# A planned order for the first tile, fewer masks, and one run of matmuls for the steps of rows 16 apart

## The chip, the core and the metric

The kernel runs on one core of one Trainium2 chip. The metric is the device time of one execution in microseconds (us); lower is better. Before the change it is 602.31 us, the median of three runs (602.05 to 604.03).

## What is computed

Two blocks follow each other. The first is a linear recurrence (RWKV-6) over 768 steps for 4 batches times 8 heads with 48 channels each; the second is a two-layer network with an exact GELU.

```python
for t in range(768):                       # r, k, v, w: (4, 8, 768, 48)
    cur = einsum('bhd,bhe->bhde', u * k[t], v[t])
    y[t] = einsum('bhd,bhde->bhe', r[t], state + cur)
    state = w[t][..., None] * state + einsum('bhd,bhe->bhde', k[t], v[t])
x = y reshaped to (3072, 384)
h = x @ w_in                               # 384 x 2048
out = (0.5 * h * (1 + erf(h / sqrt(2)))) @ w_out    # 2048 x 384
```

The two weights arrive as 64-bit floats, carried as 64-bit integers, and are turned into 32-bit floats on the chip.

## The kernel before

**Tiles.** The 3072 rows are eight tiles of 384 rows (half a sequence of one batch). `attention(x, unit)` makes the recurrence of tile x, `mlp(x)` its network. Both are Python generators: each `yield` ends a piece of work. While the network of tile x-1 fills TensorE, the recurrence of tile x is woven in between its matmuls. The instructions of every engine run in the order in which the generators are advanced; nothing reorders them. For tiles 1 to 7 that order is a string of letters, `PLAN[x]`: "." advances `mlp(x - 1)`, "s" the recurrence of tile x, "f" that of the tile after it, "l" loads, "c" the weight conversion, "w" masks and sums of weights, "x" sums of the network's input. After the string the streams are run to their ends.

**Tile 0** has no network to lie under. It is cut into two units (two pairs of heads each), `units[0]` and `units[1]`, that are advanced in turn by loops at the end of the kernel function, with matmuls on zeros (`keep_warm`, L240) between. A unit multiplies the decays w of neighbouring steps into totals (`tot_sb`, L427); then at each of six levels h = 1, 2, 4 to 32 it makes products of k and r on TensorE (`d`, L468), scales r and k by the totals on VectorE (L515, at the last level L508), and copies the wanted part of the products into `a_sb` through a mask (L527) or, for h of 16 and 32, with ScalarE (L524). At level 1 the diagonal is made too (`diag`, from r times u by ScalarE, L417; its copy is L479). The blocks of k are then transposed (`kt_ps`, L680), products of k and v made (`kv_ps`, L706), the states chained on VectorE (L726, L721), and y is the sum of two groups of matmuls (`y_ps`, L747 and L791); small copies called fences (L757, L759) stand between those two. y goes to `xT`, the input of the network (L798, L814), in part by small DMAs (L821). Tile 1 does the same steps with one unit.

**Loads.** `load_first` (L166) brings r, k and w of tile 0: per unit one DMA for r and k (768 KB) and one for w (384 KB). `weight_in` (L219, L214) brings a piece of weights, `load_second` (L178) tile 1 in eight parts; a one-element memset on VectorE (L218, L177) ahead of each part holds the DMA back to its place in the order. All of these are issued by SyncE.

**Weight conversion.** There are 16 pieces. ScalarE makes two halves of each (L345, L346, in `prepare`), VectorE finishes it (L357, L359, L361, L365, in `finish`). Five raw pieces fit.

**Masks.** Early in the kernel VectorE makes masks for the levels h = 1, 2, 4, 8, 16 and for the diagonal (L254 to L262, tensor_scalar and compare); GpSimd makes index patterns (`iota`), clears `a_sb` (L266) and the two state buffers (L270), makes the identity, and later lays out `places` (L296 to L301). Masks for `quarters` (h = 4 and 16) are made in tile 1.

**Tiles 2 to 7** use `quarters()`: two levels, h = 4 and h = 16, each with 12 blocks made in three bursts of 5, 5 and 2 (L596). A burst takes one of two pairs of PSUM banks, so the third waits until the first is copied out. At h = 16 the copies are ScalarE's (L612, six a burst). Then r is scaled (L637), k is scaled (L644, L648), k is transposed in blocks on VectorE (L547) and moved by twelve small DMAs (L542), and `kv_ps` follows. Two more PSUM banks, `bank_u`, belong to `mlp`: its first layer accumulates in them (`u_ps`, L925). The first layer of the network is L1051 for tiles 0 and 1 and L925 later, the second layer L1197 for tile 0 and L1065 later.

Of the kernel before, what the change touches and what calls it, by code (L numbers as in the profile page):

```python
# [20 lines left out]
C = 64  # L21
# [9 lines left out]
FINE = 4  # L31
# [6 lines left out]
PLAN = {  # L38
    1: (
        "ccsc.cs...c.c.csccc.cs.sccc.l.csccccssc.cccs.c..cccs.sc.ccslcsc.scsclc.c.scssl.clc.wcsc.cc"  # L40
        "wsc.l.cs.cclcc.cc.wlwlcc.c.cwcs...wwfs..w...wfwl...s.w..f..wfw...wffffffffw"
    ),
    2: (
        ".......s.l.wsslw.swssss.s.s.sss.lssls.ssssssw..s.swl..w..ww.s.w.s.sslls.ll.slf.wfs..f.xxx."
        ".xx"
    ),
    3: (
        "ss.l....ss.ss...ls.sl.....s..s....sss.s..ss.ssss.ssl...ssls..ssss..ss...s.s..ls..sl..sslls"
        "f.s..fsf.fl.f.xx..xfxx"
    ),  # L50
    4: (
        "...s.s..ss...sl.s..s..l.ssl.ss.ssss.s.s.ss...sss..sssls.s.sls...s.s.l...slsls...sl.sf.fs.f"
        "xxx.lx...x"
    ),
    5: (
        "s.sl....s.s...slss...s.s.l...s....ssls.sls..s.ssssl.ss...ss.s.ss.sss..s.s.....s.ssls.s.l.l"
        "sf.s.ffs.ff..xx..xfxxl"
    ),
    6: (
        ".s..slss.......s.s.s...sll.ssls.sssssl..s.ss...sss..sssss....ssl..ss....slsss...lsl.sf...f"  # L60
        "xxl.xf..xx"
    ),
    7: (
        "s.s.s.s....s..ss.s...s...s.....ss.ss.s.ss.sss.ss...sss..ss.sssss.......s.s..sss.s..s.s...x"
        "xx..xx"
    ),
# [8 lines left out]
def kernel(  # L75
# [83 lines left out]
    def load_first():  # L159

        t = bufs[0]
        loaded[0] = [None, None]
        size = 3 * NP * T // units_of(0)
        for i in range(units_of(0)):
            for a, b in ((0, size * 2 // 3), (size * 2 // 3, size)):
                nc.sync.dma_start(out=t[:, i * size + a:i * size + b], in_=rkw[0, :, i * size + a:i * size + b])  # L166
# [37 lines left out]
    raws = []  # L204

    def weight_in(gate=False):

        if len(raws) < len(pieces):
            dst, src = pieces[len(raws)]
            raws.append(cv.tile([128, PIECE], I64, name="raw", bufs=AHEAD) if wide else None)  # L210
            if wide:
                dst = raws[-1].rearrange("p (a c) -> p a c", a=dst.shape[1])
            if not gate:
                nc.sync.dma_start(out=dst, in_=src)  # L214
                return
            for i in range(dst.shape[1]):
                if wide:
                    nc.vector.memset(dst[:, i].bitcast(U32)[:, 0:1], 0)  # L218
                nc.sync.dma_start(out=dst[:, i], in_=src[:, i])  # L219
                yield  # L220

    nc.sync.dma_start(out=u_sb, in_=u)
# [22 lines left out]
    masks = {h: const.tile([128, C // 2], U8, name=f"mask{h}") for h in LEVELS[:-1]}  # L245
# [5 lines left out]
    s_qs = {h: q_ints[0][:, i * C:(i + 1) * C] for i, h in enumerate((1,) + QUARTERS)}  # L251
# [3 lines left out]
    for h in LEVELS[:-1]:  # L255
# [9 lines left out]
    a_sb = const.tile([128, 2, NPART * NI, C], F32, name="a_sb")  # L265
    nc.gpsimd.memset(a_sb, 0.0)  # L266
# [8 lines left out]
    quarter = {h: [const.tile([128, (3 - a) * C // 4], U8, name=f"quarter{h}_{a}") for a in range(3)] for h in QUARTERS}  # L275
# [4 lines left out]
    for i, h in enumerate(QUARTERS):  # L280
# [38 lines left out]
    def conversion():  # L319
# [10 lines left out]
        for _ in weight_in():  # L330
            pass
# [5 lines left out]
    def prepare(upto):  # L337
        if not wide:
            return
        for i in range(len(halfway), min(upto, len(raws))):  # L340
# [28 lines left out]
    def attention(x, unit):  # L369
# [91 lines left out]
        def products(bs, right, width):  # L461
            d = pair("d")
            n = 0
            for b in bs:
                for i in range(NI):
# [5 lines left out]
                    n += 1  # L471
            return d[:, :, 0:n * width]
# [10 lines left out]
        def halves():  # L483

            for h in LEVELS:
                m = C // 2 // h
                if np_ < NPART:

                    d = products(range(np_), lambda z, b, i, p: rc[z, b, i, p], C)
# [8 lines left out]
                if x == 1:  # L498
                    yield
# [841 lines left out]
```

## Time and profile before

| | before |
|---|---|
| median of the runs | 602.31 us |
| profiled execution | 603.68 us, of it 601.8 us from the first to the last instruction (the span) |
| TensorE busy | 587.2 us (98%), x7442 |
| VectorE busy | 459.9 us (76%), x878 |
| ScalarE busy | 261.3 us (43%), x604 |
| GpSimd busy | 8.4 us (1%), x24 |
| DMA | 46.79 MB, mean 78 GB/s |

In the profile PE is TensorE, PEld its weight load, DVE VectorE, ACT ScalarE, POOL GpSimd, SP SyncE. A 32-bit float matmul of the program is two instructions in the trace, so a count of 96 for L468 is 48 matmuls. The ends of matmuls are modelled: whether TensorE works at its full rate is better seen from the chain of work that ended last, which gives each run of matmuls its time.

### The profile page before, as it was taken

What the parts mean: (1) busy time and instruction counts of PE and PEld (TensorE: products, weight loads), DVE (VectorE), ACT (ScalarE), POOL (GpSimd) and SP (SyncE); (2) the same over time, 40 slices, a digit from 0 to 9 for tenths busy, and PEclk for the clock granted to TensorE, in tenths of its full rate; (3) what the DMA queues carried; (4) which work ended last, traced back from release to release, by engine and by line L of the source; (5) the groups of instructions that cost most, each with busy time, mean ns of one, the idle gap of its engine ahead of it and who ended that gap; (6) DMA issues with size and microseconds to landing.
All of it is one profiled execution on the core that took longest, in us unless ns stands there. A gap on an engine that the chain in (4) does not pass through costs nothing.

```text
span 601.8 us, 17215 instructions
## 1 busy us (share of the span) xinstructions
PE 587.2 (98%) x7442; PEld 514.3 (85%) x7442; DVE 459.9 (76%) x878; ACT 261.3 (43%) x604; POOL 8.4 (1%) x24
## 2 busy tenths in 40 slices
PE   8879999999999999999999999999999999999997
PEld 4566666656699999999999999899999999989997
DVE  8979999998878977798857968798857979631211
ACT  2346656033433545245742554235652456225510
POOL 3100000000000000000000000000000000000000
PEclk9989999999999999999999999999999999999999
DMA  5739564120053101440052210413033100300000
GB/s 199 221 115 365 178 211 125 67 76 19 3 128 116 37 21 17 122 123 19 2 120 83 64 53 5 117 47 113 2 60 94 43 1 1 68 28 6 0 14 26
DMA packets 50571, 46.79 MB, mean 78 GB/s; under 512 B 31680, under 2 KB 35904, under 8 KB 50496
## 3 DMA queue, kind: packets, MB, share of 16 engines
q1 hardware_dynamic: 50400, 45.62, 25.0%
q8 instruction: 58, 0.95, 0.7%
q14 instruction: 17, 0.14, 0.1%
q10 hardware_dynamic: 96, 0.07, 0.1%
HBM read 36.24 MB, written 4.72 MB: 68 GB/s over the span
## 4 chain that ended last, share of the span: by engine, by line
PE 91%; DVE 2%; SPq 2%; issue 2%; DMA 1%; ACT 0%; DVEq 0%; ACTq 0%
PE o_ps L1065 27%; PE h_ps L925 16%; PE u_ps L925 13%; PE h_ps L1051 11%; PE o_ps L1197 5%; PE d L596 5%; PE d L468 3%; PE y_ps L791 2%; PE kv_ps L706 2%; PE y_ps L747 2%; PE u_ps L1065 2%; PE warm L240 2%; SPq L542 1%; SPq L821 1%; PE d L589 1%
## 5 line engine op out<-in xcount | busy, mean ns | idle before, releaser
L925 PE MATMUL h_ps<-xT,w_in_sb 128*128 128x192 f32 x480 | 96.3, 331 | 1.4 <-DVE o_sb L1162 0.8
L925 PEld LDWEIGHTS h_ps<-xT,w_in_sb 128*128 128x128 f32 x480 | 79.6, 190 | 5.3 <-DVE o_sb L1162 1.5
L1051 PE MATMUL h_ps<-xT,w_in_sb 128*128 128x384 f32 x192 | 64.5, 491 | 0.0
L1051 PEld LDWEIGHTS h_ps<-xT,w_in_sb 128*128 128x128 f32 x192 | 35.7, 190 | 23.6
L612 ACT COPY a_sb<-d 32x320 f32<-32x320 f32 (+5 forms) x108 | 39.2, 363 | 3.5 <-PE d L596 1.7
L1065 PE MATMUL o_ps<-w_out_sb,g 128*128 128x192 f32 x224 | 40.0, 327 | 0.0
L1065 PEld LDWEIGHTS o_ps<-w_out_sb,g 128*128 128x128 f32 x224 | 36.8, 190 | 0.6
L925 PE MATMUL u_ps<-s,w_in_sb 128*128 128x192 f32 x192 | 35.1, 326 | 0.0
L1197 PE MATMUL o_ps<-w_out_sb,g 128*128 128x384 f32 x96 | 32.9, 493 | 0.0
L925 PEld LDWEIGHTS u_ps<-s,w_in_sb 128*128 128x128 f32 x192 | 31.9, 190 | 0.0
L1054 ACT ACTIVATE g<-h_ps 128x384 f32<-128x384 f32 (+1 forms) x32 | 14.0, 436 | 40.3 <-PE h_ps L1051 40.3
L817 ACT COPY ysb<-y_ps 128x384 f32<-128x384 f32 x8 | 3.8, 480 | 60.9 <-PE y_ps L791 48.5
L1125 DVE TENSOR_TENSOR u<-o_ps,p 128x192 f32<-128x192 f32 x7 | 2.5, 358 | 36.0 <-PE o_ps L1065 36.0
L596 PE MATMUL d<-kx,rkw 64*64 64x96 f32 x1152 | 29.9, 247 | 0.0
L596 PEld LDWEIGHTS d<-kx,rkw 64*64 64x64 f32 x1152 | 24.9, 133 | 5.7 <-issue 3.2
L721 DVE SCALAR_TENSOR_TENSOR st<-st,tot_sb,kv_ps 128x48 f32<-128x48 f32 x160 | 29.0, 258 | 0.6 <-PE kv_ps L706 0.4
L979 DVE TENSOR_TENSOR g<-g,o_sb 128x384 f32<-128x384 f32 x24 | 13.2, 549 | 21.2 <-ACT o_sb L961 21.2
L1065 PE MATMUL o_ps<-w_out_sb,f 128*128 128x192 f32 x160 | 29.1, 331 | 0.0
L1065 PE MATMUL o_ps<-w_out_sb,e 128*128 128x192 f32 x160 | 28.5, 329 | 0.0
L1065 PE MATMUL o_ps<-t,g 128*128 128x192 f32 x160 | 28.4, 330 | 0.0
L468 PEld LDWEIGHTS d<-rkw 64*64 64x64 f32 x1152 | 18.7, 134 | 10.9 <-issue 3.9
L1065 PE MATMUL o_ps<-t,s 128*128 128x192 f32 x160 | 27.9, 327 | 0.0
(164 smaller groups left out, 1213.2 us busy)
## 6 DMA issues: line engine op xcount, KB each, us to landing
rkw<-in_rkw_dram SPq DMA_DIRECT2D x54, 256.0 KB, 3.5
raw<-in_w_out_dram SPq DMA_DIRECT2D x8, 768.0 KB, 4.5
v_in<-in_v_dram SPq DMA_DIRECT2D x8, 584.0 KB, 4.1
raw<-in_w_in_dram SPq DMA_DIRECT2D x5, 768.0 KB, 7.8
out_dram<-o_sb SPq DMA_DIRECT2D x20, 192.0 KB, 2.1
rkw<-kx SPq DMA_DIRECT2D x72, 48.0 KB, 2.1
raw<-in_w_in_dram SPq DMA_DIRECT2D x9, 256.0 KB, 3.4
rkw<-in_rkw_dram SPq DMA_DIRECT2D x8, 288.0 KB, 3.5
```

The lines of the kernel that those rows point to most:

```text
L240: nc.tensor.matmul(t, lhsT=zeros[:, 0:128], rhs=zeros, start=True, stop=True)
L468: nc.tensor.matmul(d[half[p], g, n * width:(n + 1) * width], lhsT=kc[half[g], b, i, p], rhs=right(half[g], b, i, p), start=True, stop=True)
L596: nc.tensor.matmul(d[half[p], g, i * 3 * C // 2:(i + 1) * 3 * C // 2], lhsT=kc[half[g], n // NI, n % NI, p], rhs=rx[half[g], 2 * n + p], s ...
L612: nc.scalar.copy(out=at[z, :, first:behind, (a + 1) * h:], in_=d[z, :, :, o:o + (3 - a) * h])
L706: nc.tensor.matmul(kv_ps[half[g], p, i * D:(i + 1) * D], lhsT=k_t(b, i, p, g), rhs=vs(b, i, g)[half[p], 0:D], start=True, stop=True)
L721: nc.vector.scalar_tensor_tensor(out=stq[:, q, c], in0=stq[:, q, c - 1] if c else b4[:, q, NC - 1], scalar=totq[:, q, c:c + 1], in1=kvs[q ...
L925: nc.tensor.matmul(o, lhsT=lhsT, rhs=rhs, start=start, stop=True, skip_group_check=True)
L979: nc.vector.tensor_add(g_of(q, 0, 1), g_of(q, 0, 1), z)
L1051: nc.tensor.matmul(h_ps, lhsT=w_in_sb[:, f // FI, j, f % FI * 128:(f % FI + 1) * 128], rhs=xT[:, j, :], start=(j == 0), stop=(j == NJ - 1))
L1054: nc.scalar.activation(out=gs[group][:, f % FG, 0:t], in_=h_ps[:, 0:t], func=AF.Gelu)
L1065: nc.tensor.matmul(o, lhsT=lhs(j), rhs=rhs(j), start=start and j == 0, stop=(j == HF - 1), skip_group_check=True)
L1197: nc.tensor.matmul(o, lhsT=block(i, f // HF, f % HF), rhs=w_out_sb[:, f, :], start=(f == 0), stop=(f == NF - 1))
```

## The change

- The loads of tile 0 come as w, r, k for each unit, 384 KB each; u is loaded after the first w.
- The loads of tile 1 and of the first three pieces of weights, both units of tile 0 and the conversion of weights become streams of a new string, `PLAN[0]`, in place of the loops. In it "." and "s" are the two units, "c" the conversion. The strings of tiles 1 to 7 are all replaced.
- `halves` yields more often in tile 0; at level 1 of tile 0 the scaling of r and of k are two instructions. The `keep_warm` of tile 0's loops moves into `products` (two after each).
- The masks for h = 16 and the quarter masks for h = 16 are no longer made. A one-element memset of `a_sb` on VectorE after the masks makes GpSimd's clearing of `a_sb` wait for them.
- In tiles 2, 3, 5 and 7 the level h = 16 of `quarters` has bursts of 4, 4 and 4 blocks, one right after the other; the third goes into the two banks of `bank_u`, and is copied out bank by bank (12 copies in place of 6, `copy_rows`).

```diff
 PLAN = {
+    0: "llllllllllllll.ls..s...cssssc...s.ss.s.ss..sssls..csss..lcscs...s.ssccc.scc.s.s..wssc.",
...
-            for a, b in ((0, size * 2 // 3), (size * 2 // 3, size)):
-                nc.sync.dma_start(out=t[:, i * size + a:i * size + b], in_=rkw[0, :, i * size + a:i * size + b])
+            for part in (2, 0, 1):
+                s = slice(i * size + part * size // 3, i * size + (part + 1) * size // 3)
+                nc.sync.dma_start(out=t[:, s], in_=rkw[0, :, s])
+                if i == 0 and part == 2:
+                    nc.sync.dma_start(out=u_sb, in_=u)
...
-    masks = {h: const.tile([128, C // 2], U8, name=f"mask{h}") for h in LEVELS[:-1]}
+    masks = {h: const.tile([128, C // 2], U8, name=f"mask{h}") for h in LEVELS if h < 16}
...
     a_sb = const.tile([128, 2, NPART * NI, C], F32, name="a_sb")
+    nc.vector.memset(a_sb[:, 0, 0, 0:1], 0.0)
     nc.gpsimd.memset(a_sb, 0.0)
...
-    for i, h in enumerate(QUARTERS):
+    for i, h in enumerate(QUARTERS[:1]):
...
+            if x == 0 and not rest:
+                keep_warm(2)
             return d[:, :, 0:n * width]
...
+                elif x == 0 and h == 1:
+                    update(r)
+                    yield
+                    update(k)
                 else:
                     nc.vector.tensor_mul(rk, rk, tt)
...
+                    d = [bank_u(i) for i in range(2)] if spare else pair("d")
...
+                last = h == QUARTERS[-1]
+                whole = last and (x == 2 or x % 2 == 1)
+                cuts = (0, n_b // 3, 2 * n_b // 3, n_b) if whole else (0, 5, 10, n_b)
                 parts_of = list(zip(cuts, cuts[1:]))
                 ds = [burst(*parts_of[0])]
-                yield
+                if not whole:
+                    yield
                 ds.append(burst(*parts_of[1]))
+                if whole:
+                    ds.append(burst(*parts_of[2], spare=True))
                 yield
                 copy_quarters(*parts_of[0], ds[0])
                 yield
-                ds.append(burst(*parts_of[2]))
-                yield
+                if not whole:
+                    ds.append(burst(*parts_of[2]))
+                    yield
...
+        if x == 0:
+            streams = {
+                ".": units[0], "s": units[1], "f": following, "c": pieces_of_w, "w": next_v(), "x": warm(),
+                "l": chain(weight_in(0, True), islice(second, 5), weight_in(1, True), second, weight_in(2, True)),
+            }
```

## The prediction

> **What bounds the kernel now.** First the page's rows of slices: is one engine full, and where is it not?
>
> ```profile
> PE   8879999999999999999999999999999999999997
> DVE  8979999998878977798857968798857979631211
> PEclk9989999999999999999999999999999999999999
> ```
>
> TensorE is full but for the first three slices (45 us) and the last. A busy matmul row can hide waiting, so I went next to the chain of work that ended last, in order of time, at the end of the first tile:
>
> ```profile
> 34.73 2.60 issue
> 37.34 0.68 PE kv_ps L706 x17
> ...
> 41.34 1.38 PE y_ps L791 x40
> 42.72 1.40 PE warm L240 x6
> 44.12 1.53 PE d L468 x96
> 45.66 2.13 PE h_ps L1051 x6
> ```
>
> The network starts at 45.66. From there the chain is one matmul run after another: 128x384 rows at 0.33 us (54 instructions in 17.41 us), 128x192 rows at 0.162 (12 in 1.95). TensorE's waits after 44 us add up to only 3.8 us: 1.6 for the moved blocks of k, 1.4 for L1162 and L1188, 0.4 for L1110, 0.4 issue. So the time is the moment at which the network starts, plus a fixed amount of matmul work, plus little.
>
> What sets that moment? The stretch from the first scaling of tile 0 to the last fence, and VectorE's own waits in it (columns of the first: length, then busy time of PE, PEld, DVE, ACT, POOL):
>
> ```profile
> 9.38:41.06 31.68, 27.06 (x856) 18.75 (x854) 26.27 (x73) 10.35 (x20) 2.87 (x5) 0.95 0.51 162
> ```
>
> ```profile
> DVE st L726 <- PE kv_ps L706: 2.8, 2, 1.7
> DVE rkw L508 <- PE d L468: 1.3, 2, 0.8
> DVE rkw L515 <- PE d L468: 1.0, 2, 0.8
> DVE fence L757 <- PE y_ps L747: 0.8, 1, 0.8
> ```
>
> VectorE works 26.27 of 31.68 us and idles 5.4, always for TensorE. Tile 1 (45 to 126 us) has both engines full: VectorE is 4.9 of each 5 us busy there, mostly with conversion.
>
> **The change, part by part.** The sums are made against the profiled execution (603.68 us, span 601.8, 1.9 around it); the median of the runs is 602.31, and I carry the difference over to that.
>
> *Start of tile 0.* Masks: until 4.6 us every tensor_scalar on VectorE ends when a GpSimd memset ends, after that it takes 0.2:
>
> ```profile
> 1.08 1.38 POOL L266 MEMSET a_sb<- 128x1536 f32 x1
> 2.40 2.20 POOL L270 MEMSET st<- 128x1168 f32 x2
> 2.54 1.02 DVE L258 TENSOR_SCALAR p<-f 128x64 int32<-128x64 int32 x1
> 4.81 0.22 DVE L258 TENSOR_SCALAR p<-f 128x64 int32<-128x64 int32 x1
> 15.67 2.49 POOL L301 COPY rkw<-ident 32x128 f32<-32x128 f32 x4
> 16.91 0.95 DVE L515 TENSOR_TENSOR rkw<-rkw,tot_sb 128x768 f32<-128x768 f32 x1
> ```
>
> The new memset holds GpSimd back, so twelve mask operations and the diagonal's (start to start 0.16 each, as from 4.81 on) end at about 3.5 us in place of 6.4, three of the old ones being dropped. Behind GpSimd's new wait stand the state buffers' clearing, the index patterns and the identity: `a_sb` is clear at 5.0 (first copy into it at 10), the identity ready at 9 (kt at 29), so nobody waits for them. Fourteen one-element memsets follow on VectorE (0.06 each, 0.8) and let fourteen DMAs of weights and tile 1 go at once, behind the first tile's in SyncE's queue. The first w, now ahead of all, is 384 of 2,304 KB; at the 400 GB/s of that stretch it lands at about 4.5. Totals (0.56 + 1.32 = 1.88): first unit 4.6 to 6.5; second w (fourth of six parts) lands at about 7.3, its totals end at 9.2. r and k of unit 0 land at about 6.5, so d and diagonal (0.9 each, no zeros between) end at 8.3, hidden behind the totals. First scaling at 9.2 against 9.38, with both totals done. r and k of unit 1 land at 9.3; wanted at 12.
>
> GpSimd's copies (L301, four of 0.62) move from 15.7 to about 10, beside scalings with two inputs. [...]L515 at 16.91 took 0.95 inside the copies, 0.97 elsewhere. I take nothing, and keep up to 2.5 for the range.
>
> *VectorE to the last fence.* 26.27 busy, less the second totals, now ahead (12.22 to 14.06: 1.84), plus what the new order brings in of conversion: one L365 (0.95) and a second piece (L357, L359, L361, L365: 0.56 + 0.56 + 0.95 + 0.95 = 3.02), overlaps off 3.85; plus 0.30 for the split at level 1 (four of 0.554 for two of 0.96). Sum 28.6. From 9.2 this ends at 37.8, if the conversion falls where VectorE idled. It is placed so: after the masks of level 8, between L508s, ahead of L726. The tightest place is behind the last k scaling: kt (0.75 a unit), its ScalarE copy (0.81) and kv (0.84) take 2.4 us and hand-overs, while VectorE has 1.9 (three steps of a piece, start to start), 0.5 (r of one unit) and 0.9 (L365) = 3.3 us of other work. ScalarE makes pieces 0 and 1 (4 us) ahead of the level 16 copies (wanted near 23): the second raw piece must have landed by 19; at 300 to 400 GB/s it lands at 17 to 20, so this just holds. Before, the fence ended at 41.3: 3.5 gained.
>
> Two deductions. The 2.60 us "issue" wait above is an instruction stream that ran dry: the DMAs stayed near 90% until 35.0 and then moved under 20 GB/s until 37. Now the loads are finished near 22 us, so it can fall elsewhere. It made VectorE wait 1.7. Bounds 0 and 2.6; I take half of 1.7: 0.9. The clock: after that idle it was halved.
>
> ```profile
> 37.00:38.00 1.00, 0.67 (x21) 0.66 (x22) 0.00 (x0) 0.00 (x0) 0.00 (x0) 0.50 0.00 0
> ```
>
> In the new order TensorE is ahead of VectorE here: about 1.8 us idle before the first half of L791 and 1.2 before the second, 0.7 of work between, no zeros. [...]By the row (2.6 us idle, then 0.50 in each slice from 37 to 40) y, zeros and the first d lose up to 1.6. I take 0.5[...]. Then y 1.38, zeros 1.40, d 1.53 follow as before. The small DMAs of xT stand behind two pieces of weights and v on SyncE; v waits for the first group of y, which by this count ends near 34, before xT's data (37): no cost. **Start: 3.5 - 0.9 - 0.5 = 2.1 us.**
>
> *Tile 1.* Matmuls are the same. VectorE enters it 1.4 pieces further on, and 0.6 us of quarter masks are gone: it stays off the path. If that lead were lost, each late piece would stop L1051 at once.
>
> *One run.* In tiles 2, 3, 5, 7 the level h = 16 goes from two runs to one; the built order also shows tile 6's first level with one run of 40 matmuls for two of 20.
>
> ```profile
> 227.18 1.81 PE d L596 x80
> 228.99 2.80 PE o_ps L1065 x16
> 231.78 0.49 PE d L596 x16
> ```
>
> (1.81 - 0.49)/64 is 0.0206 an instruction, so 16 need 0.33 and entering costs 0.16; the sixteen o_ps after it take 2.80 where 8 take 1.30 (2.60): 0.20 for leaving. 0.36 x 5 = **1.8 us**, all on TensorE's path.
>
> *Waits.* In the same tiles r and k no longer wait for a third burst behind 8 o_ps (2.6 us), so the twelve moves of k start some 2 us sooner: the 1.6 us of kv_ps waiting for them (1.1 at 383 us) go. ScalarE has six more copies of about 0.33 in each of these tiles, 19 us ahead of y_ps, at 43% load: no cost. The third burst needs bank_u, whose last reader (GELU, about 364.0 in tile 5) ends before the burst at 364.7. I leave the other 2.2 us as they are. **1.6 us.**
>
> Sum 2.1 + 1.8 + 1.6 = 5.5: span 596.3, **median 596.8 us**.
>
> **The rivals.** *A, the start gains nothing*: [...]a dry stream that VectorE sees in full (2.6). For it: the old wait; against: loads end early. no 2.1, and the 0.5 of the clock lost: 602.31 - 3.4 + 0.5 = 599.4. *B, no deductions and fewer waits*: 3.5, 1.8, and waits 1.6 + 1.4 (L1162 and L1188 too) make 8.3: 594.0. *C, new orders cost what they save*: the strings of tiles 1 to 7 are all new, and VectorE is 98% busy in tile 1; some 5 us of waits would bring 602.3. *D, slower*: the fourteen early DMAs share the engines with the first tile's instead of following it. All 7.7 MB at 410 GB/s would land together near 19 us; unit 1 is wanted at 12, so VectorE stops 7 us: 5.5 - 7 gives 603.8. It decides from a landing at 17.5 on. Against it: before, parts landed in the order of issue (r and k at 5.78, w by 6.67, the next at 8.57). That the one run doesn't come about is no rival: the order of the built kernel has it.
>
> **How the numbers follow.** Likeliest 0.58 (own range 594.8 to 598.6), A 0.18, B 0.14, C 0.05, D 0.05. Range 593.4 to 600.0: it takes in A and most of B. 0.3% (1.8 us) is about what a measurement here can tell from no change; C alone lies within it: faster 0.90, same 0.05, slower 0.05.
>
> **What would show it.** Masks ending near 3.5; first scaling near 9.2; two pieces converted before the last fence, that near 38.7 (before 41.3); L1051 starting near 43.5 (45.66); 96 instructions of L596's successor in one entry of about 2.1 us in tiles 2, 3, 5, 7; no kv_ps wait for moved blocks. It is wrong if TensorE shows "issue" or a half clock for long before 45 us, or waits of over 2 us in tile 1.

## The result, and the profile after

The changed kernel takes **598.95 us** (median of five runs, 597.18 to 600.46); the kernel before took 602.31 beside it. The ratio is 0.9939, with a 95% interval of 0.9911 to 0.9968: 3.4 us faster by the medians, 3.7 by the ratio. The forecast was 596.8, its range 593.4 to 600.0. So the sign and the range held, and the likeliest value missed by 2.2 us. The profiled execution took 600.21 us (span 598.4), 1.3 above the median of its kernel, as the one before stood 1.4 above its own; profile against profile the difference is 3.5 us, so the two can be set side by side.

The time is not where the forecast put it. First the slices of the page:

```profile
PE   5779999999999999999999999999999999999997
DVE  7799999998969967798858978698868979531211
PEclk9899999999999999999999999999999999999999
```

TensorE starts emptier than before (5, 7, 7 in place of 8, 8, 7), and the clock is down in the second slice. The chain of the work that ended last (start, length, what) shows why, up to the start of the network:

```profile
17.97 0.91 PE d L471 x45
18.89 2.44 issue
21.33 0.33 PE d L471 x3
...
37.36 0.68 PE kv_ps L728 x46
38.04 3.39 issue
41.42 0.20 PE kv_ps L728
...
44.04 1.38 PE y_ps L814 x38
...
47.10 1.53 PE d L471 x96
48.63 2.13 PE h_ps L1072 x6
```

There are now two stretches of "issue", 2.44 and 3.39 us, where there was one of 2.60. In each of them TensorE stands in the middle of a run of matmuls whose operands are there. The network starts at 48.63, where the forecast had about 43.5 and the kernel before 45.66: **3.0 us later, not 2.1 sooner**. From that start to the last instruction of the span the program needs 549.8 us, where it needed 556.1: **6.4 us less**, where the forecast had 3.4 (one run 1.8, waits 1.6). Both halves were off, in opposite directions.

VectorE in the first tile, from the timeline of its instructions (start, length, line, operation, idle before it and what ended that):

```profile
3.03 0.22 DVE L264 TENSOR_TENSOR mask<-f 128x64 uint8<-128x64 int32 x1
...
4.00 0.56 DVE L430 TENSOR_TENSOR tot_sb<-rkw 128x384 f32<-128x384 f32 x1 [0.47 <-DMA rkw<-in_rkw_dram]
...
8.28 0.56 DVE L430 TENSOR_TENSOR tot_sb<-rkw 128x384 f32<-128x384 f32 x1 [2.37 <-DMA rkw<-in_rkw_dram]
8.88 1.31 DVE L430 TENSOR_TENSOR tot_sb<-tot_sb 128x192 f32<-128x192 f32 x5
10.13 1.03 DVE L513 TENSOR_TENSOR rkw<-rkw 128x384 f32<-128x384 f32 x2
```

The masks end at 3.25 us, a quarter of a microsecond ahead of the forecast. The w of unit 1 lands at 8.26, where 7.3 was forecast, so the first scaling is at 10.13 and not at 9.2. From there to the last fence, as a window (length; busy time of PE, PEld, DVE, ACT, POOL; clock; DMA share; GB/s), and VectorE's waits in it (total, times, longest):

```profile
10.13:43.99 33.86, 23.67 (x831) 18.41 (x842) 28.57 (x62) 13.59 (x24) 2.85 (x5) 0.90 0.56 196
```

```profile
DVE rkw L524 <- PE d L471: 3.8, 4, 1.9
DVE st L748 <- PE kv_ps L728: 1.1, 1, 1.1
DVE rkw L513 <- PE d L471: 0.2, 1, 0.2
```

VectorE's work is 28.57 us; the forecast had counted 28.6. It idles for another 5.3 us, 5.1 of it for TensorE. From the fence at 43.99 the network starts 4.64 us later (forecast: 4.8).

Behind the start, TensorE's waits from 44 us to the end:

```profile
PE y_ps L814 <- DVE fence L779: 0.5, 1, 0.5
PE u_ps L1086 <- ACT u_ps L1131: 0.4, 1, 0.4
PE h_ps L946 <- DVE o_sb L1183: 0.2, 1, 0.2
```

The first of these lies ahead of the start. So of the 3.8 us of waits that followed 44 us before, 0.6 is left. The one run of h = 16 in tile 3, from the chain:

```profile
228.82 1.48 PE d L605 x64
230.30 0.66 PE u_ps L605 x32
230.96 5.07 PE o_ps L1086 x30
```

It is 96 instructions in one entry of 2.14 us (forecast: about 2.1); the last 32 bear the name `u_ps`, since they go into the banks of `bank_u`.

### The profile page after: what moved, and what is told of

Its sections match the earlier page's. It is cut to its first block, busy times and chain, and to the rows that moved or that the text cites. A ratio compares the mean times of both kernels' runs of the same rounds, so it can differ in the third digit from the quotient of the medians.

```text
span 598.4 us, 17186 instructions
## 1 busy us (share of the span) xinstructions
PE 579.1 (97%) x7410; PEld 512.4 (86%) x7424; DVE 455.7 (76%) x875; ACT 264.4 (44%) x628; POOL 8.0 (1%) x21
## 4 chain that ended last, share of the span: by engine, by line
PE 94%; DVE 2%; issue 2%; DMA 1%; SPq 1%; ACT 0%; DVEq 0%; ACTq 0%
PE o_ps L1086 30%; PE h_ps L946 16%; PE u_ps L946 13%; PE h_ps L1072 11%; PE o_ps L1218 5%; PE d L605 4%; PE d L471 4%; PE kv_ps L728 2%; PE y_ps L814 2%; PE y_ps L769 2%; PE u_ps L1086 2%; PE d L597 1%; DMA rkw<-in_rkw_dram 1%; PE warm L240 1%; SPq L844 1%
## 5 line engine op out<-in xcount | busy, mean ns | idle before, releaser
L946 PE MATMUL h_ps<-xT,w_in_sb 128*128 128x192 f32 x480 | 95.0, 330 | 0.2 <-DVE o_sb L1183 0.2
L471 PEld LDWEIGHTS d<-rkw 64*64 64x64 f32 x1152 | 20.1, 142 | 15.2 <-issue 10.8
L621 ACT COPY a_sb<-d 32x256 f32<-32x256 f32 (+8 forms) x84 | 30.5, 363 | 5.2 <-PE d L605 3.8
L1218 PE MATMUL o_ps<-w_out_sb,g 128*128 128x384 f32 x96 | 32.5, 491 | 0.0
L638 DVE COPY_PREDICATED a_sb<-quarter,d 128x480 f32<-128x480 uint8 (+5 forms) x54 | 23.1, 438 | 11.8 <-PE d L605 10.6
L471 PE MATMUL d<-rkw 64*64 64x64 f32 (+1 forms) x1152 | 22.5, 230 | 7.0 <-issue 2.8
L1086 PE MATMUL o_ps<-t,g 128*128 128x192 f32 x160 | 28.6, 330 | 0.0
L1086 PE MATMUL o_ps<-t,e 128*128 128x192 f32 x160 | 28.4, 328 | 0.0
```

The costliest lines, as they stand in the source:

```text
L471: nc.tensor.matmul(d[half[p], g, n * width:(n + 1) * width], lhsT=kc[half[g], b, i, p], rhs=right(half[g], b, i, p), start=True, stop=True)
L621: nc.scalar.copy(out=at[z, g, first:behind, (a + 1) * h:], in_=d[z, :, :, to] if g == slice(None) else d[z, :, to])
L638: nc.vector.copy_predicated(out=an[:, :, :, :, (a + 1) * h:], mask=mask.to_broadcast(data.shape), data=data)
L946: nc.tensor.matmul(o, lhsT=lhsT, rhs=rhs, start=start, stop=True, skip_group_check=True)
L1086: nc.tensor.matmul(o, lhsT=lhs(j), rhs=rhs(j), start=start and j == 0, stop=(j == HF - 1), skip_group_check=True)
L1218: nc.tensor.matmul(o, lhsT=block(i, f // HF, f % HF), rhs=w_out_sb[:, f, :], start=(f == 0), stop=(f == NF - 1))
```

## The experiments

Two questions had to be settled: what the start is worth, and what the gain behind the start is made of. Each result below is a median with its extremes, and the ratio to the kernel before measured beside it (602.1 to 602.5 in all of them).

### What the parts are worth

**The one run alone.** The kernel before with the bursts of 4, 4 and 4, the old strings, the old start and the old masks.

```diff
+                whole = last and (x == 2 or x % 2 == 1)
+                cuts = (0, n_b // 3, 2 * n_b // 3, n_b) if whole else (0, 5, 10, n_b)
                 ds.append(burst(*parts_of[1]))
+                if whole:
+                    ds.append(burst(*parts_of[2], spare=True))
```

> The kernel before with only the part on rows 16 apart: bursts of 4, 4 and 4, the third in the two banks of bank_u and right behind the second, in tiles 2, 3, 5 and 7; the number of steps is kept, so that the old strings still fit. If entering and leaving a run costs 0.36 us on TensorE's path, and the moved blocks come sooner, it is 4 x 0.36 = 1.4 us plus 1.6 us of kv_ps waits faster: 602.3 to 599.3 us. If only the runs count: 600.9. If neither is on the path (the new strings made the gain behind the start): 602 to 602.6.

Measured: 600.62 us (599.02 to 603.77), ratio 0.9966 [0.9952, 0.9979]: 1.9 us gained. In its waits the moved blocks of k are still there:

```profile
PE kv_ps L719 <- DMA rkw<-kx: 1.8, 4, 0.8
```

This run has four of the five entries that the forecast counted (1.4 us at 0.36 each), and 1.4 lies within its interval (1.3 to 2.9 us). In its profile the stretch from the network's start to the end of the span is 1.8 us shorter, 0.6 of it in shorter waits, which leaves about 1.2 for the four entries. The rest of the 1.9 is not settled: the profile also has a shorter issue wait ahead of the network. The run does not take the wait for the moves away. That has to come from the strings.

**The old start with all the rest.** The new strings of tiles 1 to 7, the fewer masks of `quarters` and the one run, but the loads, the masks ahead and the loops of tile 0 as before.

```diff
-            for part in (2, 0, 1):
+            for a, b in ((0, size * 2 // 3), (size * 2 // 3, size)):
...
-        "cscs.scc.csc..csc.scw.c.cclcscc.lsc.sscsc.c.lcscw.cccc.sc.cc.wcsc.s.c.ccsccsc.s.ll.c.scccc"
+        "cccscs.scc.csc..csc.scw.c.cclcscc.lsc.sscsc.c.lcscw.cccc.sc.cc.wcsc.s.c.ccsccsc.s.ll.c.scccc"
```

> The first tile, its loads and its order as before the change (masks of level 16 included), with the new strings of tiles 1 to 7 and the one run: the rest of the change without its start. Two steps of the conversion that the new first tile had made stand at the head of tile 1's string instead, and tile 1's first step too. Theory 1 (the change loses some 3 us at the start and gains 6 behind it): network start 44 to 46 as before, 549.5 to 551 from there to the end of the span, time 595.5 to 597.5, faster than both kernels. Theory 3 (the gain behind the start was bought by the conversions and loads that the new first tile had already done): from network start to the end 553 or more, time 599 to 601.

Measured: 600.88 us (598.39 to 604.20), ratio 0.9970 [0.9952, 0.9987]. Tiles 2 to 7 take 467.2 us of it, as in the changed kernel (467.2; before 472.3, from the start of tile 1's network to TensorE's end), and of the wait for moved blocks 0.4 is left there. But the edit made a wait of its own: three conversions stood ahead of the first step of tile 1, and ScalarE stood in the conversion, waiting for its raw piece, while TensorE wanted `kx`:

```profile
PE d L465 <- ACT kx L414: 2.3, 1, 2.3
```

So one letter was moved ahead of the conversions (`sccccs.scc` for `cccscs.scc`).

> Edit: the old start of tile 0 with the new strings and the one run, as in the run of the old start before it, but with one 's' of tile 1's string moved ahead of its first three 'c', so that k's copy on ScalarE (L414) no longer stands behind a conversion whose raw piece lands late. Theory 1 (the new start is a loss of about 2 us, and the run of the old start hid that behind 2.3 us of waiting for this copy): tiles 0 and 1 together come to about 126 us again (126.1 before the change, 128.0 after it), tiles 2 to 7 stay at 467.2, span about 596.5, time 596.5 to 598, faster than the changed kernel (598.95). Theory 2 (tile 1 needs the new start's lead in conversion, and without it another wait comes up): tiles 0 and 1 stay near 128, time 599.5 to 601.

Measured: **598.89 us** (598.61 to 600.49), ratio 0.9950 [0.9932, 0.9968]. The profile is as theory 1 had it: tile 1's network starts at 125.8 (128.0 after the change), span 596.8. The median is not: it lies 0.9 above the 596.5 to 598 expected, and beside the changed kernel's 598.95. With the old start the network begins at 43.1 in this profile, but tile 1 then loses what was won: TensorE waits 2.4 us for a GELU on ScalarE that stands behind the conversion, a wait that the changed kernel does not have.

```profile
PE h_ps L1062 <- ACT g L1065: 2.4, 2, 1.8
```

**What follows.** By the medians, the one run gives 1.9, the new strings another 1.7 (600.62 to 598.89), and the new start nothing (598.89 to 598.95). By the ratios, each taken to the kernel before beside it, the same steps are 2.0, 1.0 and 0.7. The intervals leave each of them uncertain by a good microsecond; that the new start gives nothing is shown no better than that. The forecast had 1.8, 1.6 and 2.1. In the profiles the old start looks better by 2.2 us at the start of tile 1's network (125.8 beside 128.0), but 1.5 of that is the two executions' own distance from their medians (0.3 below, 1.3 above).

### What the two issue waits are

The first of the two stretches begins at the same instruction in the kernels below that load as the changed one does: behind 349 matmuls and 349 weight loads (with more zeros, late pieces, u first, data left out; the changed kernel's trace shows 345 and 349, with some records missing). The second lies about 1,024 matmuls and weight loads later (1,705 counted at 38.04). In the kernel before, its one wait lies at about the same place (1,723 counted at 34.73). That speaks for certain places in TensorE's stream of instructions. The page has a DMA queue named "instruction" (58 packets, 0.95 MB in both kernels), and my reading, which the runs below test, is that the stream runs dry there and TensorE stands until a packet of this queue has landed. The packets are set beside the waits at the end of this part. The DMA engines were full at the first:

```profile
12.00:16.00 4.00, 3.45 (x97) 2.83 (x98) 3.75 (x6) 0.89 (x2) 1.47 (x4) 0.57 1.02 378
16.00:20.00 4.00, 2.60 (x102) 1.80 (x97) 3.75 (x5) 0.96 (x2) 1.38 (x2) 1.00 1.05 373
```

(DMA share 1.02 and 1.05; the kernel before has 0.16 and 0.72 in these two windows.)

**The loads spread over the steps.** Each load of tile 1 and of the weights stands between steps of tile 0, instead of fourteen at once.

```diff
-    0: "llllllllllllll.ls..s...cssssc...s.ss.s.ss..sssls..csss..lcscs...s.ssccc.scc.s.s..wssc.",
+    0: ".s..s...lsslsslc..l.sl.sslc.sl.ssl..slssls.l.cssls..lcscls.l.l.s.sslccc.scc.s.s..wssc.",
```

> The changed kernel with the seventeen load steps of the first tile's string spread over it (three weight parts, three more, then the eight parts of tile 1, then the last three) instead of fourteen at its head; nothing else. Theory 1 (TensorE's instruction stream is refilled by the same DMA engines, at the same place in the stream in both kernels, and the refill stands behind data): the issue wait of 2.4 us in the products near 19 us goes; the one of 3.4 us in the second run of kv_ps stays, since two weight pieces of 768 KB are still issued ahead of it. The network starts 1 to 3 us sooner than the 48.6 us of the changed kernel, 45.5 to 47.5, and the time is 596 to 598. Theory 2 (the start is late through the order w, r, k and the halved clock, whatever the other loads do): network start 48 to 49, time 598.5 to 599.5.

Measured: 599.45 us (597.76 to 600.04), ratio 0.9946 [0.9928, 0.9965]. The first wait is gone, the DMA share in 12 to 16 us is 0.23, and VectorE waits for no product of k and r any more. The second became longer, and the time is the same:

```profile
PE kv_ps L728 <- issue: 4.3, 1, 4.3
```

```profile
34.40:38.70 4.30, 0.01 (x2) 0.01 (x2) 2.58 (x14) 0.00 (x0) 0.00 (x0) 0.75 1.01 378
```

The engines are full in that stretch too (share 1.01): the spread loads now reach into it.

**Pieces 3 and 4 later.** Their two loads of 768 KB are held back from 32.5 and 37 us until tile 1, and two steps of conversion go from tile 0's string to tile 1's; then the same with the spread loads.

```diff
+        if holding[0]:
+            postponed.append(i + 3)
+            return
...
+            for i in postponed:
+                for _ in weight_in(i):
+                    pass
```

> The changed kernel with the DMAs of weight pieces 3 and 4 issued after the first tile instead of at 32.5 and 37 us, and the first step of the third conversion moved into tile 1. Theory 1: the issue wait in the second run of kv_ps (3.4 us) shrinks below 0.5, that near 19 us stays; the network starts at 45.5 to 47, the time is 596 to 598. Theory 2: no change in either (48 to 49; 598.5 to 599.5).

> Both edits at once. Theory 1: neither issue wait is over 0.5 us before the network starts; it starts at 43 to 45 us (the predicted 43.5 was made with 0.9 for such a wait), and the time is 593.5 to 596. Theory 2: 598 to 599.5.

Measured: 603.48 us (601.42 to 606.01), ratio 1.0016 [0.9997, 1.0035], and 601.16 (599.70 to 605.13), ratio 0.9979 [0.9964, 0.9994]. In the first, the wait at `kv_ps` is down to 1.2 us, but the pieces now come too late: ScalarE waits at the conversion of piece 3, with tile 1's `kx` behind it, and TensorE waits 4.1 us for that. With both edits the wait at `kv_ps` is 3.2 again: pieces 3 and 4 are out of its way, but the spread loads of piece 2, issued at 31.6 to 32.5, are not (DMA share 0.83 in 32 to 36 us). Another 2.6 us go at `kx`. So the wait follows the data that is there, and the data cannot simply be moved later: the time came back at another place.

```profile
PE d L475 <- ACT kx L424: 4.1, 1, 4.1
PE d L475 <- issue: 2.6, 2, 1.8
PE kv_ps L732 <- issue: 1.2, 1, 1.2
```

**More zeros.** Twelve zero matmuls at first in place of eight, and six behind each diagonal in place of two, to keep the clock up. It asks whether the clock, and not the stream, sets the start.

> The changed kernel with more matmuls on zeros at its start: 12 in place of 8 ahead of the first products, and 6 in place of 2 behind each unit's diagonal. Theory 1 (TensorE stands still in the first 12 us for want of zeros, its clock is halved at 12 to 16 us, and VectorE waits 3.8 us for slow products): the clock stays at 1.00 from 10 to 16 us, VectorE's waits on products near 20 to 27 us fall below 2.5, the network starts 1 to 2 us sooner than 48.6, time 597 to 598. Theory 2 (only the two issue waits count, the clock is hidden): network start 48 to 49, time 598.5 to 599.5.

Measured: 599.46 us (598.98 to 601.48), ratio 0.9942 [0.9922, 0.9962]. The clock in 10 to 15 us is 1.00 in place of 0.74, the two waits are 2.3 and 3.0, the network starts at 49.7. The clock of that stretch is not what was lost. (Behind the first of the two waits it fell in this kernel too, to 0.50 from 22 to 24 us; what that costs was not tested.)

```profile
10.00:15.00 5.00, 4.10 (x140) 2.73 (x133) 4.79 (x12) 1.12 (x2) 0.00 (x0) 1.00 1.03 394
```

**Zeros, spread loads, and pieces 3 and 4 at a chosen place:** first near the end of tile 0's string (a letter "p" that issues both), then right behind the first chain of states.

```diff
-    0: ".slll..s...clllssssc...s.ss.lsl.lslsl.l.lslslslls..csss..cscs...s.ssccc.sc.s.s..wsps.",
+    0: ".slll..s...clllssssc...s.ss.lsl.lslsl.l.lslslslls..csss..cscs...s.ssccc.sc.sp.s..wss.",
```

> The changed kernel with the zeros of the run before the last, and with its loads paced: three load steps behind the totals, three after level 1, the eight of tile 1 from level 4 on, weight piece 2 after them, pieces 3 and 4 only behind the last state chain; the third conversion starts in tile 1, behind the first step of its recurrence. If theory 1 on the refills and the zeros holds: no issue wait over 1.5 us, clock 1.00 up to 35 us, network start 42.5 to 45, time 593.5 to 596. If the two edits hide each other or pieces 3 and 4 come too late for ScalarE: 597 to 600.

> Edit: the changed kernel with tile 0's loads spread over the steps (two ahead of the rest, the others one by one between them), 12 zero matmuls first and 6 behind each diagonal, and raw pieces 3 and 4 issued together right behind the first chain of states (about 39 us) instead of as soon as a raw buffer is free (32.5 and 37). Theory 1 (the loss at the start is TensorE's instruction stream waiting behind data in the DMA engines, at fixed places of the stream near its 700th and 1,720th instruction; with the engines free there nothing is lost): no issue wait over 1.5 us before 45 us, no wait for ScalarE at the conversion of pieces 3 and 4, network starts at 44 to 46, time 595 to 597.5. Theory 2 (the waits are no matter of the data beside them): issue waits of 2 to 3.5 at both places again, network starts at 48 to 49, time 599 to 599.5.

Measured: 599.20 us (597.65 to 601.08), ratio 0.9939 [0.9916, 0.9963], and 601.98 (600.46 to 604.50), ratio 0.9996 [0.9981, 1.0011]. With the late place the wait at `kv_ps` is 0.6, those at d 2.7 (two, the longer 1.6, where no more than 1.5 was expected), the network starts at 45.2, and tile 1 waits 2.4 us for a GELU behind a conversion; the time is the one expected for pieces that come too late. With the early place no single issue wait is over 1.4 us, which is what theory 1 asked for, and yet the network starts at 48.6, as theory 2 had it. Neither theory had named the reason: the two pieces, issued at about 39 us, are ahead of the small transfers of `xT`, which now need 4.7 us from issue to landing (median; 3.5 in the changed kernel), and the first layer waits for those.

```profile
PE h_ps L1076 <- DMA xT<-ysb: 2.5, 1, 2.5
PE kv_ps L732 <- issue: 1.8, 2, 1.4
PE y_ps L818 <- issue: 1.3, 1, 1.3
```

**The data left out.** The loads of pieces 3 and 4, and then of 1 to 4, are dropped, and their raw tiles are set to zero once on GpSimd.

```diff
+            if i in LEFT_OUT:
+                for _ in range(3 if gate else 0):
+                    yield
+                return
...
+        if i in LEFT_OUT:
+            nc.gpsimd.memset(raws[i].bitcast(F32), 0.0)
```

> Edit: the changed kernel with the loads of the raw weight pieces 3 and 4 left out; GpSimd sets their raw tiles to zero once, near 9 to 11 us, so that the conversion and everything else still run with zeros in place of these two pieces of w_in. What is left out are two of the transfers (768 KB each, issued at 32.5 and 37 us in the changed kernel). Theory 1 (the 3.39 us for which kv_ps has nothing to execute at 38 us is TensorE's instruction stream standing behind this data): that wait falls below 1 us, the network starts 2 to 3 us sooner, at 45.5 to 46.5, and the wait near 19 us stays at 2 to 3; time 596 to 597.5. Theory 2 (the wait comes with that place of the stream whatever the DMA engines do): it stays at 2.5 to 3.5, start 48 to 49, time 598.5 to 599.5.

> Edit: as the run with the loads of pieces 3 and 4 left out, and the loads of pieces 1 and 2 (issued among and behind those of tile 1 at the start) left out too, their tiles set to zero once by GpSimd before 15 us. Theory 1: with 1.5 MB less in the queues the loads of tile 1 are through near 18 us, so that the wait near 19 us shrinks as well (below 1.5 us), VectorE's waits for the products before 44 us shrink from 4.0 to about 2, the network starts at 43.5 to 45, which is what the prediction forecast for the changed kernel, and the time is 594 to 596.5. Theory 2: waits of 2 to 3.5 us at both places again, start 47.5 to 49, time 598 to 599.5.

Measured: 598.91 us (598.17 to 599.23), ratio 0.9940 [0.9919, 0.9961], and 597.24 (595.39 to 599.33), ratio 0.9911 [0.9887, 0.9935]. The wait at `kv_ps` falls from 3.39 to 1.2 in both, while the DMA engines are idle (share 0.00 to 0.04), and the network starts at 46.8 and 46.4 (the two windows are from the first of the two kernels):

```profile
35.00:38.00 3.00, 2.77 (x147) 2.43 (x146) 2.96 (x6) 2.88 (x5) 0.00 (x0) 1.00 0.02 5
38.00:40.00 2.00, 0.97 (x50) 0.83 (x49) 2.00 (x11) 1.76 (x3) 0.00 (x0) 1.00 0.00 0
```

This lies between the theories, nearer to the first. With the engines empty the second wait is 1.2; with late pieces it was 1.2 as well, and with full engines it was 3.0 to 4.3. So data on the engines makes some 2 to 3 us of it, and 1.2 stays without any. The first wait stays at 2.1 even with 1.5 MB less to load: the DMA share in that stretch is 0.13, but in the 4 us from 12 to 16 it is still 1.04, and from 16.0 to 18.4 us 1.00.

```profile
18.56:20.65 2.09, 0.01 (x2) 0.01 (x2) 1.50 (x2) 0.00 (x0) 0.00 (x0) 1.00 0.13 49
```

So theory 1's "below 1.5" failed here: with these pieces gone the engines were still full up to the wait. What took the first wait away was the spreading, with idle time in the engines well ahead of it. And in the medians leaving out pieces 3 and 4 brought nothing that can be measured (598.91 beside 598.95); leaving out four pieces brought 1.7 us, with intervals that still overlap.

**u first.** The load of u ahead of the first w, as before the change.

```diff
+        nc.sync.dma_start(out=u_sb, in_=u)
-                if i == 0 and part == 2:
-                    nc.sync.dma_start(out=u_sb, in_=u)
```

> Edit: the changed kernel with the load of u issued first, as before the change, instead of behind the first w. Theory 1 (the second w, landing at 8.26 us where 7.3 was forecast, is late because u's many small packets sit in the queues ahead of it): w of unit 1 lands at about 7.3, the first w some 0.5 later than 4.0, first scaling near 9.5 (10.13 after the change); time 598 to 599, as the later waits take most of it. Theory 2 (it is late because r, k and the two w simply need that long at this rate): it lands at 8.2 to 8.6 again, first scaling 10.1 to 10.6, time 599 to 599.5.

Measured: 599.29 us (596.26 to 600.96), ratio 0.9939 [0.9914, 0.9964]. The totals of unit 1 start at 8.6 and the first scaling at 10.5. Theory 2 holds: u is not what makes the second w late.

### All starts side by side

TensorE's issue waits ahead of the network (d, `kv_ps` and `y_ps`, from 3 us on) and the first matmul of the network, from each profile, in us:

| | issue waits | network starts | difference |
|---|---|---|---|
| before | 2.6 | 45.6 | 43.0 |
| one run alone (old start) | 0.8 | 44.4 | 43.6 |
| old start, new strings | 2.1 | 44.8 | 42.7 |
| old start, steps first | 0.3 | 43.1 | 42.8 |
| **after** | **6.2** | **48.6** | **42.4** |
| spread loads | 4.3 | 47.1 | 42.8 |
| late pieces | 3.8 | 47.1 | 43.3 |
| spread loads, late pieces | 3.5 | 45.8 | 42.3 |
| more zeros | 5.3 | 49.7 | 44.4 |
| u first | 6.5 | 49.3 | 42.8 |
| zeros, paced loads | 3.3 | 45.2 | 41.9 |
| the same, pieces early | 4.0 (and 2.5 for `xT`) | 48.6 | 44.6 (42.1 without `xT`) |
| no pieces 3, 4 | 4.0 | 46.8 | 42.8 |
| no pieces 1 to 4 | 3.7 | 46.4 | 42.7 |

Over waits from 0.3 to 6.5 us the difference stays near 42.8 (41.9 to 44.4 with the wait for `xT` taken off; a line through the points rises by 0.99): a microsecond of these waits is a microsecond of the start. And it is the same for the old start and the new one. The new order of tile 0 does not bring the network forward even without these waits, and in these profiles it has more of them. One caution: the table has one execution of each kernel, and those of the changed kernel, of more zeros, u first and the paced loads took 1.3 to 2.0 us more than the medians of their kernels.

### The packets of the instruction queue

The waits can be set beside the transfers. From the page of the changed kernel, and from its DMA queues between 38.90 and 40.00 us (packets, MB, share of the 16 engines):

```profile
q8 instruction: 58, 0.95, 0.7%
q8 instruction: 1, 0.02, 5.7%
```

Each of the 58 packets has 16 KB. Some of them and the waits, in us:

| | stream dry at | packet | TensorE goes on at |
|---|---|---|---|
| before | 34.73 | 34.91 to 35.84 | 37.34 |
| after, first | 18.89 | 18.98 to 19.93 | 21.33 |
| after, second | 38.04 | 38.95 to 39.96 | 41.42 |
| spread loads | 34.38 | 36.48 to 37.46 | 38.69 |
| no pieces 3, 4 (second) | 37.77 | 36.60 to 37.53 | 38.96 |
| no pieces 1 to 4 (first) | 18.56 | 18.40 to 19.35 | 20.64 |
| no pieces 1 to 4 (second) | 37.35 | 36.16 to 37.26 | 38.53 |

In the fourteen traces there are 28 issue waits of 0.4 us or more ahead of the network. Every one ends 2.2 to 2.5 us after the start of such a packet, 1.2 to 1.6 us after its end. And they begin not at two places but at six: behind 449, 705, 1,217, 1,473, 1,729 or 1,985 records of TensorE (its few other records counted with the matmuls and weight loads; the changed kernel's trace lacks some records and has 701 and 1,717); the others lie 256 records, or a multiple of that, behind the first. My reading is that TensorE stands at such a place when the packet comes late; what a packet holds the traces do not show. The experiments show what goes with a late one: with pieces 3 and 4 on the engines (the changed kernel) the packet at the second place starts 0.9 us after TensorE has run dry (38.95 beside 38.04), without them 1.2 us before (36.60 beside 37.77).

## Why the prediction was right, and where it was wrong

That the time lies in the forecast range is in part luck. In the profiles the network starts 5.1 us later than forecast, and what follows takes 3.0 us less than forecast; the two errors cancel in the main.

- **Masks: right.** 3.5 was forecast, 3.25 measured; `a_sb`, the identity and the index patterns were waited for by nobody.
- **First loads: wrong by 0.96.** The second w was to land at 7.3 by the rate of 400 GB/s; it landed at 8.26, and its totals start at 8.28, with u first at 8.6. In 5 to 10 us the engines moved 380 GB/s, but over the first 5 us only 177.
- **GpSimd's copies beside the scalings: the cost right, the reading of the row too coarse.** Nothing was lost on VectorE. The four copies were read as one row of 2.49 us; taken singly, three take 0.40 to 0.42 us and the fourth 1.1, in the kernel before (1.12) as in the changed one. From the copies of the changed kernel (shortest, median, longest in ns) and the timeline of VectorE:

```profile
L304 POOL COPY rkw<-ident x4: 401/409/1107, 15.0 to 16.3; 32x128 f32<-32x128 f32 x4
16.19 0.94 DVE L524 TENSOR_TENSOR rkw<-rkw,tot_sb 128x768 f32<-128x768 f32 x1
```

The fourth copy starts at 16.31, just behind the start of the scaling with two inputs, and ends at 17.42, 0.29 us after it. In the kernel before it starts at 17.03, 0.12 us behind such a scaling, and ends at 18.15, also 0.29 us after it. The scaling beside the copy took 0.94 us, the next one, at 17.86 with no copy beside it, 0.98. So the copy took longer and the scaling did not; why was not shown. Nobody waits for these copies.

- **VectorE to the last fence: the work right, the deduction wrong.** 28.6 us of work was forecast and 28.57 measured, with two pieces converted ahead of the fence. This is the step that failed: "I take half of 1.7: 0.9" for the stream that ran dry, with "Bounds 0 and 2.6". TensorE stood for 5.8 us on the path (2.44 and 3.39) and VectorE for 5.1. The forecast had the cause right by my reading of the packets: each of these waits ended 1.4 to 1.5 us behind the end of one. Two errors are in the size. The wait of before was priced by what VectorE was seen to wait (1.7), while the table shows that all of it moves the start. And the upper bound was that of one wait, while the order now had two: the profile of before showed one place of the stream where it ran dry, and I did not ask where the other packets of the stream would fall, once the loads came as one block.
- **What hid it.** The sum without the deductions was a start of 42.1; the late w puts 0.9 on that, which makes 43.0, and the table has 42.8 for most of the new starts. But the same table puts the old start, without its waits, at 43.0. The 3.5 us of gain were thus measured against a kernel whose 2.6 us of waiting were counted as part of its order.
- **The clock: 0.5 for a loss that did not come where it was put.** Behind the long wait it stayed at 1.00; it fell to 0.50 behind the first one, and with more zeros, where it was 1.00 from 10 to 15 us in place of 0.74, the kernel was not faster (599.46 us beside 598.95). The work ahead of each fall is in the last section.
- **Tile 1 off the path: right, and it was worth something.** It was put at no gain. In the profiles the stage from the start of tile 0's network to that of tile 1's takes 79.3 us, before 80.5, and 82.7 where the old start with steps first has less conversion behind it. The lead in conversion is what the new start does bring, and by the medians it about pays for the waits.
- **One run: the mechanism right, the count one too high.** 1.8 was forecast for five entries, but the traces have only four fewer: from 127 us on TensorE goes from the network into other products 42 times before and 38 times after. In tile 6 two runs of 40 and 72 instructions became two of 80 and 32, so no entry is saved there. The four alone gave 1.9 by the medians and about 1.2 in the profile, where 1.4 was forecast for them.
- **Waits: the right size in the medians, another cause.** 1.6 forecast, 1.7 measured as the step from the one run alone to the new strings (1.0 by the ratios). I had tied the end of the `kv_ps` wait to the bursts; alone they left it at 1.8. It is the new strings that end it. In the profiles the strings also took the waits at L1162 and L1188 and for an issue, of which rival B had counted 1.4. From the start of tile 1's network to TensorE's end 5.1 us are gone: the listed waits fall from 3.4 to 0.6, the four entries are worth about 1.2, and some 1.1 us stand in no wait of the list.
- **The rivals.** A, "the start gains nothing", at 599.4, is what came about (598.95), through a dry stream seen in full. B's waits came, its start did not. C, new strings that cost what they save, fell: tiles 1 to 7 have no wait above 0.4 us. D, loads that share the engines, was near in its mechanism: w of unit 1 came in the order of issue, as argued against D, so no step stood 7 us for its data, but the block of loads is what comes before the first dry stream.

**Open:** what sets the start of a packet when the engines are idle. The 1.2 us of the second wait that stay without pieces 3 and 4 are its arithmetic: the packet starts 1.2 us before the stream is dry, and TensorE goes on 2.4 us after that start. But why it starts no sooner (4.9 us after the packet before it, where 3.3 us is the least in any of the traces) is not known. The 2.1 us that stay at the first place have data ahead of them: the engines are full up to 18.4 us, and the packet starts at 18.40. The old order passed that place without a wait; its packet came at 13.6 us, when its loads left the engines idle (0.16 in 12 to 16 us).

## What to carry to other kernels

When a profile shows an "issue" wait in the middle of a run of matmuls, count the engine's instructions up to it, and look at the packets of the instruction queue. In the reordered kernel it can come again at that count, and at others: here the waits began 256 records of TensorE apart, or a multiple of that, and most such places are passed without a wait. Price it in full on the path of the engine that stands (here a line of slope 0.99), and ask what is on the DMA engines at that time: the block of loads issued early because "nothing waits for it" kept the engines at a share of 1.02 to 1.05 from 12 to 20 us, TensorE stood for 2.44 us from 18.89, and with the loads spread (0.23 in 12 to 16 us) that wait was gone. Idle engines shortened the second wait here (3.39 to 1.2 us without pieces 3 and 4), they did not end it. And before you credit a new order with a gain, take the old order's accidental waits off its time.

## What was not expected of the hardware

- TensorE's issue waits of 0.4 us or more ahead of the network began behind six counts of its records only, 256 or a multiple of that apart, though the same count (1,729) was reached at times from 34.4 to 38.5 us; the time lost at one of them was between 0 and 4.3 us.
- The clock did not follow the length of the idle time. Behind the wait of 2.44 us (18.89 to 21.33, the changed kernel) it fell to 0.50; behind that of 3.39 us (38.04 to 41.42) it stayed at 1.00. In the profiles of the two kernels it is 0.50 in three stretches ahead of 50 us: 36.99 to 40.40 us before the change, 12.37 to 15.78 and 22.61 to 26.02 after it. Each is 3.41 us long, and the last two start 10.24 us apart, three times that. From windows of the changed kernel of this length, cut at these moments (length, busy time of PE first, the clock third from the end):

```profile
8.96:12.37 3.41, 1.56 (x65) 1.11 (x63) 3.24 (x9) 1.12 (x2) 0.00 (x0) 1.00 1.04 398
12.37:15.78 3.41, 3.08 (x90) 2.46 (x91) 3.19 (x5) 0.67 (x1) 1.31 (x3) 0.50 1.02 374
...
19.20:22.61 3.41, 1.14 (x36) 0.79 (x41) 1.47 (x3) 1.78 (x2) 0.00 (x0) 1.00 0.76 273
22.61:26.02 3.41, 3.05 (x82) 2.16 (x74) 2.14 (x5) 0.00 (x0) 0.00 (x0) 0.50 0.02 6
...
36.26:39.67 3.41, 1.78 (x122) 1.65 (x115) 3.37 (x13) 3.41 (x5) 0.00 (x0) 1.00 0.77 291
39.67:43.09 3.42, 1.67 (x82) 1.66 (x83) 2.28 (x13) 0.30 (x1) 0.00 (x0) 1.00 0.02 5
43.09:46.50 3.41, 2.83 (x59) 2.07 (x55) 3.23 (x12) 0.61 (x2) 0.00 (x0) 1.00 0.63 198
```

Behind windows with 1.56 and 1.14 us of work the clock is 0.50; behind those with 1.78 and 1.67 us, across which the long wait lies, it is 1.00. In the kernel before, too, 1.15 us of work from 33.58 to 36.99 us stand ahead of the 0.50. That is what two profiles show; no run changed the work in a window alone, so whether it is the work that the clock follows was not shown.
